# Sixteen units of a soft-routed MoE layer: the gated tile turned by a DMA transpose in f16 words instead of by TensorE in f32

## The chip, the cores and the metric

The kernel runs on one core of one Trainium2 chip. The metric is the device time of one execution in microseconds (us). The kernel before was timed three times: 547.62, 548.83 and 551.03 us, median 548.83 us. TensorE is called PE, VectorE DVE, ScalarE ACT, GpSimd POOL, and the queue on SyncE from which nearly all transfers are issued SP.

## The reference

Three layers follow one another, all in float32. Causal attention with decay over 4 batches x 8 heads x 576 positions x 64 gives x of 2304 tokens x 512. Layer 1 is a dense feed-forward layer with a sigmoid gate, and layer 2 a soft mixture of 8 experts with 4 slots each:

```python
h = x @ w_in                                  # 2304 x 2048
g = h * (1.0 / (1.0 + np.exp(-1.702 * h)))
y = g @ w_out                                 # 2304 x 512
logits = y @ phi                              # 2304 x 32
d = softmax(logits, over tokens); c = softmax(logits, over slots)
slot_input = d.T @ y                          # 32 x 512
slot_out[e] = relu(slot_input[e] @ w1[e]) @ w2[e]
out = c @ slot_out                            # 2304 x 512
```

## The kernel before, in words

**Layer 1 is folded.** y is never formed. The kernel computes `wphi = w_out @ phi` (2048 x 32) once, and the logits as `g @ wphi`; the sums over tokens are taken of g and multiplied by `w_out` at the end.

**Tiles.** The 2304 tokens are 18 blocks of 128; two blocks make a chunk, so there are nine chunks, 0 to 8. A chunk has eight units: a block `t` (0 or 1) and a group `fg` of 512 of the 2048 columns. In chunks 1 to 7 unit `u` is `t = u // 4`, `fg = u % 4`. A unit is twelve f16 matmuls of 512 columns into one PSUM bank `hp` (lines 814 to 816: high words times high, high times low, low times high, over four slices of 128), a Tanh on ACT into `g` (L829), and a multiplication on DVE (L830), which leaves the gated f32 tile `g`, 128 tokens x 512.

**The turn.** For the logits g must stand with its 512 columns on the partitions. `turn` transposes the four 128 x 128 pieces on PE in f32 against the identity (L766, `gT` in PSUM) and copies the result to SBUF on ACT (L773, `gt`, a ring of three tiles). `by_phi` then issues four f32 matmuls of `wphi` (32 columns) with `gt` (L788); each stands in the trace as two records, and piece `a` writes the partitions 32a to 32a+31 of the bank `p4`, so that four groups of PE columns are used. The 32-row groups are added up later by a matmul with `rsum` in `slot_steps`. A unit's `turn` is called in the step of the next unit or later, and its `by_phi` with the next `turn`, behind the last `hp` matmul issued.

**Attention runs between the units.** From row 5 on a piece of attention is: scores on PE (`scs`), a running maximum on DVE (L577), Exp on ACT (L581), normalisation into a high and a low f16 word, `pn`, on ACT and DVE (L589, L590), a DMA transpose from SP into `ph` (L594; most are 128x8x128, 128 partitions by eight blocks of 128), and then the products with the values on PE (`pv`, L632 to 634). Two `pn` tiles and three `ph` tiles rotate. The new row's q and k are turned by DMA transposes too (L347). `attn_items` gives each piece a place and a cost, and the main loop interleaves them with the units of layer 1 by goals; the tile framework then orders each engine's instructions by a simulated timeline. Each engine and the SP queue work strictly in that order.

**The end.** When attention's last item is issued its pool is closed and the expert weights of layer 2 are loaded from SP into the memory that has come free (L1109 onward, 127 transfers of 256 KB); PE works on chunks 7 and 8, and then on layer 2.

Of the kernel before, what the change touches and what calls it, by code (L numbers as in the profile page):

```python
# [10 lines left out]
F32 = mybir.dt.float32  # L11
F16 = mybir.dt.float16
BF16 = mybir.dt.bfloat16
U32 = mybir.dt.uint32
AF = mybir.ActivationFunctionType
# [15 lines left out]
def attention_moe_softmoe(ctx, tc, q, k, v, f, w_in, w_out, phi, w1, w2, out):  # L31
# [131 lines left out]
    w_at, w_loaded = [0], [0]  # L163
    W_AHEAD = 7

    N_LOW = 2
    RAW_AT = (7, 6, 5, 4, 3, None, None, 7, 6, None, None, 7, None, None, None, None)
    wo_pair = {}

# [28 lines left out]
    def w_first(n):  # L198


        if n in W32:
            nc.scalar.activation(out=W32[n], in_=W32[n], func=AF.Copy, scale=WS)
            return
        words = w_raw.pop(n).rearrange("p (n w) -> p n w", w=2)
        lo, hi = words[:, :, 0], words[:, :, 1]
        val = W32[n] = w32_tile(n)
        low = ap_.tile([128, 512], U32, tag="low", name="low", bufs=N_LOW)
        if n % 2 < 1:
            nc.gpsimd.tensor_scalar(out=val, in0=hi.bitcast(F32), scalar1=2.0 ** -111, scalar2=None, op0=ALU.mult)
        else:  # L210
            nc.scalar.activation(out=val, in_=hi.bitcast(F32), func=AF.Copy, scale=2.0 ** -111)
        nc.scalar.activation(out=low, in_=lo, func=AF.Copy, scale=0.93 * 2.0 ** -29)
        bits = val.bitcast(U32)
        nc.vector.scalar_tensor_tensor(
            out=low, in0=bits, scalar=3, in1=low, op0=ALU.logical_shift_left, op1=ALU.bitwise_or
        )
        nc.vector.scalar_tensor_tensor(
            out=bits, in0=bits, scalar=0x80000000, in1=low, op0=ALU.bitwise_and, op1=ALU.bitwise_or
        )
# [519 lines left out]

    G = {}
    P4 = {}
    held = deque()
# [6 lines left out]
    def units(c):  # L751
# [3 lines left out]
            return [(t, 2 * b + a) for b in range(2) for t in range(2) for a in range(2)]  # L755
        return [(t, fg) for t in range(2) for fg in range(FG)]

    def turn(c, t, fg):


        g = G[c, t, fg]
        pt = pt2 = ps_mm("gT")
        if (c, t, fg) == (NCH - 1, 1, FG - 1):
            pt2 = ps_sc("gT")
        for a in range(4):
            last_turn[0] = nc.tensor.transpose((pt if a < 2 else pt2)[:, a * 128:(a + 1) * 128], g[:, a * 128:(a + 1) * 128], ident)  # L766
        gt = mp.tile([128, 512], F32, tag="gt", name="gt", bufs=N_GT)
        if (c, t, fg) == (NCH - 1, 1, FG - 1):
            nc.scalar.copy(out=gt[:, halves[0]], in_=pt[:, halves[0]])
            nc.vector.tensor_copy(gt[:, halves[1]], pt2[:, halves[1]])  # L770
            warm(2)
        else:
            nc.scalar.copy(out=gt, in_=pt)  # L773
        with tc.issue_after(last_turn[0].ins):
            while held:
                by_phi(*held.popleft())
        held.append((c, t, fg, gt))
        if c == NCH - 1:
            by_phi(*held.popleft())

    def by_phi(c, t, fg, gt):
# [2 lines left out]
        if (t, fg) == first:  # L784
            P4[c, t if one else 0] = (ps_sc if one and t else ps_mi)("p4")
        p4 = P4[c, t if one else 0][:, 0 if one else 128 * t:][:, 0:128]
        for a in range(4):
            last_p4[0] = nc.tensor.matmul(  # L788
                p4[NS * a:NS * (a + 1)], lhsT=wphi[:, 4 * fg + a, :], rhs=gt[:, a * 128:(a + 1) * 128],
                start=((t, fg) == first), stop=(fg == FG - 1), skip_group_check=True,  # L790
# [9 lines left out]
    def moe_steps(c):  # L800
        xt = XT[c]
        for u, (t, fg) in enumerate(units(c)):
# [26 lines left out]
            nc.scalar.activation(out=g, in_=hp, func=AF.Tanh, scale=0.851 / (VS * WS))  # L829
            nc.vector.scalar_tensor_tensor(out=g, in0=g, scalar=1.0, in1=hp, op0=ALU.add, op1=ALU.mult)  # L830
            turns.append((c, t, fg))
            for _ in range(min(3 if c < 2 else 2, len(turns) - 1)):
                if turns[0][2] >= folded[0]:
                    break
                turn(*turns.popleft())
# [42 lines left out]
    def slot_steps(c, ts=(0, 1)):  # L878
# [3 lines left out]
        end = c == NCH - 1 and ts[-1] == 1  # L882
        l4 = mp.tile([128, 256], F32, tag="l4", name="l4", bufs=1)[:, 0:128 * nt]
        nc.vector.tensor_scalar(
            out=l4, in0=P4.pop((c, ts[0]))[:, 0:128 * nt], scalar1=1.0 / (GS * WS), scalar2=None, op0=ALU.mult
        )
        lg = ps_mi("lg")
        lT = lg[:, 0:128 * nt]
# [477 lines left out]
```

## Time and profile before

| | |
|---|---|
| median of three runs | 548.83 us |
| the profiled execution | 544.7 us, span of its instructions 542.2 us |
| PE busy | 492.7 us, 91% of the span |
| DVE busy | 350.4 us, 65% |
| ACT busy | 310.6 us, 57% |
| POOL busy | 71.5 us, 13% |
| granted TensorE clock, mean | 0.978 |
| bytes read from and written to HBM | 64.63 MB and 4.72 MB |

An engine's busy time is the union of its instructions in the trace. PE's matmuls are pipelined: one that lasts 0.38 us in the trace can start 0.22 us after the one before it. What a group of matmuls costs PE is therefore read from the starts: from its first start to the start of what follows. Chunks are found by the 72 Tanh instructions (L829), eight to a chunk: chunk 2's run from 189.7 to 227.3 us, chunk 4's from 272.6 to 310.5 us, chunk 6's from 364.6 to 404.9 us.

### The profile page before, as it was taken

Reading aid. Unit: us, or ns where it says so; the run is one execution under the profiler, and the core shown is the slowest. Engines: PE = TensorE matmul, PEld = TensorE weight load, DVE = VectorE, ACT = ScalarE, POOL = GpSimd, SP = SyncE. Lnnn points to the kernel's source line nnn. Section 1 sums busy time; section 2 is a strip of 40 time slices with the busy share of each in tenths; the row PEclk is TensorE's granted clock in tenths of the full one; section 3 lists DMA queues with packets and bytes.
Section 4 is the critical chain, followed back from the end, with each engine's and each line's share of the span. In section 5 each row is a group of like instructions: output and inputs, shape, how many; then the busy total and the mean of one; then the engine's idle time right before and its main releaser. Section 6 shows DMA issues by size and latency. Waiting matters only on the chain.

```text
span 542.2 us, 13552 instructions
## 1 busy us (share of the span) xinstructions
PE 492.7 (91%) x5353; PEld 309.1 (57%) x5353; DVE 350.4 (65%) x898; ACT 310.6 (57%) x607; POOL 71.5 (13%) x123
## 2 busy tenths in 40 slices
PE   3467899999889999999999999989999999999982
PEld 3456776866567555655665657556665555454531
DVE  8988979778666447667677868877675413360132
ACT  5867686778667446556666667576664323221211
POOL 4866754311000000010000001000000000000000
PEclk9969799999999999999999999999999999999997
DMA  9998763999959307997739699994554499989998
GB/s 242 285 376 149 200 129 133 272 191 204 169 105 168 61 19 139 185 181 139 125 77 181 116 189 176 212 156 88 93 105 90 132 383 367 348 308 367 337 327 269
DMA packets 230847, 105.62 MB, mean 195 GB/s; under 512 B 202593, under 2 KB 213345, under 8 KB 230785
## 3 DMA queue, kind: packets, MB, share of 16 engines
q1 hardware_dynamic: 229552, 103.59, 80.3%
q10 hardware_dynamic: 1232, 1.18, 0.7%
q8 instruction: 42, 0.69, 0.6%
q14 instruction: 21, 0.16, 0.1%
HBM read 64.63 MB, written 4.72 MB: 128 GB/s over the span
## 4 chain that ended last, share of the span: by engine, by line
PE 65%; DMA 15%; DVE 9%; ACT 4%; SPq 2%; issue 2%; POOL 0%; DVEq 0%; ACTq 0%; POOLq 0%
PE hp L814 10%; PE hp L815 9%; PE hp L816 9%; DMA ph<-pn 6%; PE gT L766 5%; PE p L788 4%; DMA we<-in_moe_w_dram 3%; PE pv L626 3%; PE l L1227 3%; PE sp L954 3%; PE pv L632 2%; DMA kf<-in_k_dram 2%; PE scs L554 2%; DMA kab<-kan 2%; PE scs L555 2%
## 5 line engine op out<-in xcount | busy, mean ns | idle before, releaser
L814 PE MATMUL hp<-w,xt 128*128 128x512 f16 x288 | 109.6, 381 | 0.6 <-DVE g L830 0.6
L815 PE MATMUL hp<-w,xt 128*128 128x512 f16 x288 | 109.2, 379 | 0.0
L816 PE MATMUL hp<-w,xt 128*128 128x512 f16 x288 | 109.2, 379 | 0.0
L581 ACT ACTIVATE pf<-scs,mx 128x512 f32<-128x512 f32 (+3 forms) x108 | 57.3, 541 | 38.7 <-DVE mx L577 29.4
L830 DVE SCALAR_TENSOR_TENSOR g<-g,hp 128x512 f32<-128x512 f32 x72 | 49.2, 683 | 43.9 <-ACT g L829 43.7
L590 DVE SCALAR_TENSOR_TENSOR pn<-pf,pn 128x512 f16<-128x512 f32 (+2 forms) x78 | 51.2, 658 | 32.1 <-ACT pn L589 31.4
L829 ACT ACTIVATE g<-hp 128x512 f32<-128x512 f32 x72 | 42.5, 590 | 47.4 <-PE hp L816 47.3
L589 ACT ACTIVATE pn<-pf 128x512 f16<-128x512 f32 (+2 forms) x78 | 47.3, 607 | 22.3 <-DMA ph<-pn 19.8
L577 DVE CUSTOM_DVE_ANT_0 scs<-scs,zmq 128x128 f32<-128x128 f32 (+3 forms) x96 | 46.6, 496 | 6.8 <-PE scs L555 4.2
L773 ACT COPY gt<-gT 128x512 f32<-128x512 f32 x71 | 41.1, 582 | 10.7 <-PE gT L766 10.5
L816 PEld LDWEIGHTS <-xt 128*128 128x128 f16 x288 | 28.2, 98 | 32.9
L632 PE MATMUL pv<-vv,ph 128*128 128x65 f16 (+1 forms) x360 | 41.8, 196 | 5.3 <-DMA ph<-pn 4.2
L814 PEld LDWEIGHTS <-xt 128*128 128x128 f16 x288 | 28.8, 100 | 28.8 <-issue 5.0
L766 PE MATMUL gT<-ident,g 128*128 128x128 f32 x288 | 45.0, 277 | 0.0
L766 PEld LDWEIGHTS gT<-ident,g 128*128 128x128 f32 x288 | 34.0, 141 | 14.8 <-issue 3.5
L632 PEld LDWEIGHTS <-ph 128*128 128x128 f16 (+1 forms) x360 | 33.8, 102 | 14.6 <-issue 7.0
L815 PEld LDWEIGHTS <-xt 128*128 128x128 f16 x288 | 28.2, 98 | 23.7 <-issue 1.1
L633 PE MATMUL pv<-vv,ph 128*128 128x65 f16 (+1 forms) x360 | 41.7, 195 | 0.0
L634 PE MATMUL pv<-vv,ph 128*128 128x65 f16 (+1 forms) x360 | 41.4, 194 | 0.0
L588 POOL MEMSET pn<- 128x128 f16 x12 | 2.5, 205 | 252.6 <-DMA ph<-pn 250.8
L633 PEld LDWEIGHTS <-ph 128*128 128x128 f16 (+1 forms) x360 | 34.1, 102 | 2.5 <-issue 0.6
L554 PE MATMUL scs<-kab,qa 128*128 128x128 f16 x240 | 34.4, 220 | 0.5 <-ACT pf L581 0.5
(233 smaller groups left out, 1017.3 us busy)
## 6 DMA issues: line engine op xcount, KB each, us to landing
we<-in_moe_w_dram SPq DMA_DIRECT2D x127, 256.0 KB, 5.5
raw<-in_moe_w_in_dram SPq DMA_DIRECT2D x16, 512.0 KB, 7.2
raw<-in_moe_w_out_dram SPq DMA_DIRECT2D x16, 512.0 KB, 5.7
kf<-in_k_dram SPq DMA_DIRECT2D x13, 256.0 KB, 3.3
qf<-in_q_dram SPq DMA_DIRECT2D x13, 256.0 KB, 3.7
vf<-in_v_dram SPq DMA_DIRECT2D x12, 256.0 KB, 4.2
out_dram<-ob SPq DMA_DIRECT2D x12, 256.0 KB, 3.5
ph<-pn SPq DMA_TRANSPOSE x78, 3.0
```

Source lines behind the costliest of these rows:

```text
L554: nc.tensor.matmul(o, lhsT=QA[r][:, h, :], rhs=KA[base + j][:, h, :], start=True, stop=False)
L577: nc.vector.tensor_tensor_reduce(out=o, in0=o, in1=mask, scale=-SC, scalar=3.0e38 if n == 128 else DG[r][1][:, u], op0=ALU.add, op1=ALU.mi ...
L581: nc.scalar.activation(out=pf[:, hh * nb:(hh + 1) * nb], in_=o, func=AF.Exp, bias=mx[:, hh:hh + 1], scale=-1.0)
L589: nc.scalar.activation(out=pn[:, 0, 0:w], in_=pf, func=AF.Copy, scale=PB)
L590: nc.vector.scalar_tensor_tensor(out=pn[:, 1, 0:w], in0=pf, scalar=PB, in1=pn[:, 0, 0:w], op0=ALU.mult, op1=ALU.subtract)
L632: nc.tensor.matmul(o, lhsT=ph[0:rr, 0, off:off + n], rhs=vh, start=(j == 0), stop=False)
L633: nc.tensor.matmul(o, lhsT=ph[0:rr, 0, off:off + n], rhs=vl, start=False, stop=False)
L766: last_turn[0] = nc.tensor.transpose((pt if a < 2 else pt2)[:, a * 128:(a + 1) * 128], g[:, a * 128:(a + 1) * 128], ident)
L814: nc.tensor.matmul(hp, lhsT=xt[:, 0, kk, ts], rhs=win(0, fg, kk), start=(kk == 0), stop=False)
L815: nc.tensor.matmul(hp, lhsT=xt[:, 0, kk, ts], rhs=win(1, fg, kk), start=False, stop=False)
L816: last_hp[0] = nc.tensor.matmul(hp, lhsT=xt[:, 1, kk, ts], rhs=win(0, fg, kk), start=False, stop=(kk == KD - 1))
L830: nc.vector.scalar_tensor_tensor(out=g, in0=g, scalar=1.0, in1=hp, op0=ALU.add, op1=ALU.mult)
```

## The change

In units 1, 2, 3, 5 and 6 of chunks 2 and 4 and units 1 to 6 of chunk 6 the turn is done another way. `stage`, called right behind the unit's L830, writes g times 2^-8 as a high and a low f16 word side by side into `gh` (one on ACT, one on DVE), and a DMA transpose from SP turns both words at once, 128x8x128, into `gt`. `turn` then issues no PE transpose and no ACT copy for that unit, but only the held `by_phi` of the unit before. `by_phi_halves` multiplies with f16 words of `wphi` (made once, `split_wphi`): two matmuls of 64 columns (g's high word with both words of wphi), four of 32 columns (g's low word with the high word of wphi), two of 64 columns. The other units of these chunks keep the PE transpose and scale by 2^-8 in the copy; the divisor in `slot_steps` takes the factor back. The two tiles of the tag `low` get tags of their own, `low0` and `low1`, which `gh` and the words of `wphi` use after them.

```diff
-        low = ap_.tile([128, 512], U32, tag="low", name="low", bufs=N_LOW)
+        low = ap_.tile([128, 512], U32, tag=f"low{n % 2}", name="low")
...
+    BY_DMA = {2: (1, 2, 3, 5, 6), 4: (1, 2, 3, 5, 6), 6: (1, 2, 3, 4, 5, 6)}
+    TS = 2.0 ** -8
+    wphl = []
+    staged = {}
...
+    def split_wphi():
+        wphl.append(ap_.tile([128, 512], F32, tag="low1", name="wphl").bitcast(F16).rearrange(
+            "p (k h s) -> p k h s", k=KF, h=2))
+        nc.scalar.activation(out=wphl[0][:, :, 0], in_=wphi, func=AF.Copy)
+        nc.vector.tensor_tensor(out=wphl[0][:, :, 1], in0=wphi, in1=wphl[0][:, :, 0], op=ALU.subtract)
+
+    def stage(c, t, fg):
+        g = G[c, t, fg]
+        gh = ap_.tile([128, 512], F32, tag="low0", name="gh").bitcast(F16).rearrange("p (h n) -> p h n", h=2)
+        nc.scalar.activation(out=gh[:, 0], in_=g, func=AF.Copy, scale=TS)
+        nc.vector.scalar_tensor_tensor(
+            out=gh[:, 1], in0=g, scalar=TS, in1=gh[:, 0], op0=ALU.mult, op1=ALU.subtract
+        )
+        gt = mp.tile([128, 512], F32, tag="gt", name="gt", bufs=N_GT).bitcast(F16)
+        nc.sync.dma_start_transpose(
+            out=gt.rearrange("p (a q) -> p a q", q=128), in_=gh.rearrange("p h n -> p (h n)")
+        )
+        staged[c, t, fg] = gt
+
+    def by_phi_halves(p4, fg, gt, stop):
+        gt = gt.rearrange("p (h a q) -> p h a q", h=2, a=4)
+        for both, a, g0 in ((1, 0, 0), (1, 1, 2), (0, 0, 0), (0, 1, 1), (0, 2, 2), (0, 3, 3), (1, 2, 0), (1, 3, 2)):
+            w = wphl[0][:, 4 * fg + a, 0:1 + both].rearrange("p h s -> p (h s)")
+            last_p4[0] = nc.tensor.matmul(
+                p4[NS * g0:NS * (g0 + 1 + both)], lhsT=w, rhs=gt[:, 1 - both, a],
+                start=False, stop=stop, skip_group_check=True,
+            )
+
     def turn(c, t, fg):
+        if (c, t, fg) in staged:
+            with tc.issue_after(last_hp[0].ins):
+                while held:
+                    by_phi(*held.popleft())
+            held.append((c, t, fg, staged.pop((c, t, fg))))
+            return
...
+        elif c in BY_DMA:
+            nc.scalar.activation(out=gt, in_=pt, func=AF.Copy, scale=TS)
...
-        for a in range(4):
+        if gt.dtype == F16:
+            by_phi_halves(p4, fg, gt, fg == FG - 1)
+        for a in range(4) if gt.dtype == F32 else ():
...
+            if u in BY_DMA.get(c, ()):
+                if not wphl:
+                    split_wphi()
+                stage(c, t, fg)
...
-            out=l4, in0=P4.pop((c, ts[0]))[:, 0:128 * nt], scalar1=1.0 / (GS * WS), scalar2=None, op0=ALU.mult
+            out=l4, in0=P4.pop((c, ts[0]))[:, 0:128 * nt], scalar1=1.0 / (GS * WS * (TS if c in BY_DMA else 1.0)),
+            scalar2=None, op0=ALU.mult
```

How the instructions move, at two places. The first is PE in chunk 6, at one of its units, before (`gT` is the PE transpose, `p` the product with `wphi`):

```order
L555 MATMUL scs<-kab,qb 128x128
L766 MATMUL gT<-ident,g 128x128 x4
L788 MATMUL p_5242<-gt,wphi 32x128 x4
L814 LDWEIGHTS xt
L814 MATMUL hp<-w,xt 128x512
```

And PE at a staged unit of chunk 2 in the changed program (`wphl` is the f16 words of `wphi`):

```order
L857 MATMUL hp<-w,xt 128x512
L784 LDWEIGHTS wphl
L784 MATMUL p_2916<-gt,wphl 64x128
L784 LDWEIGHTS wphl
L784 MATMUL p_2916<-gt,wphl 64x128
L784 LDWEIGHTS wphl
L784 MATMUL p_2916<-gt,wphl 32x128
...
L784 MATMUL p_2916<-gt,wphl 32x128
L784 LDWEIGHTS wphl
L784 MATMUL p_2916<-gt,wphl 64x128
L784 LDWEIGHTS wphl
L784 MATMUL p_2916<-gt,wphl 64x128
L564 LDWEIGHTS qa
```

The four transposes are gone, and the four f32 products have become eight f16 ones whose stationary tile changes from 64 to 32 columns and back. Over the program the PE transposes `gT` fall from 288 to 224, and 128 products with `wphl` come in. In five places other PE work now stands inside such a group of eight; the program before has two groups of `p` cut in the same chunks.

The second place is the SP queue in chunk 6, up to the first expert weights, before:

```order
L594 DMA_TRANSPOSE ph<-pn 128x6x128 x6
L347 DMA_TRANSPOSE qa<-qan 128x8x64
L347 DMA_TRANSPOSE qb<-qbn 128x8x64
L594 DMA_TRANSPOSE ph<-pn 128x6x128
L594 DMA_TRANSPOSE ph<-pn 128x8x128 x8
L594 DMA_TRANSPOSE ph<-pn 128x10x128 x4
L1109 DMA we<-in_moe_w_dram 128x512 x64
```

And in the changed program:

```order
L593 DMA_TRANSPOSE ph<-pn 128x6x128 x4
L775 DMA_TRANSPOSE gt<-gh 128x8x128
L593 DMA_TRANSPOSE ph<-pn 128x6x128 x2
L346 DMA_TRANSPOSE qa<-qan 128x8x64
L346 DMA_TRANSPOSE qb<-qbn 128x8x64
L775 DMA_TRANSPOSE gt<-gh 128x8x128
L593 DMA_TRANSPOSE ph<-pn 128x6x128 x2
L775 DMA_TRANSPOSE gt<-gh 128x8x128
L593 DMA_TRANSPOSE ph<-pn 128x8x128 x2
L775 DMA_TRANSPOSE gt<-gh 128x8x128
L593 DMA_TRANSPOSE ph<-pn 128x8x128 x3
L775 DMA_TRANSPOSE gt<-gh 128x8x128
```

The six new transposes stand one by one between attention's, and none stands behind the last `ph`, where the weights' loads begin.

## Rows read from the trace of the kernel before

**Rows 1.** Windows: length; busy us of PE, PEld, DVE, ACT, POOL; granted clock, DMA share, GB/s.

```profile
150.00:428.00 278.00, 272.33 (x3124) 166.98 (x3120) 189.97 (x526) 172.77 (x350) 5.56 (x32) 1.00 0.71 128
189.00:230.00 41.00, 41.00 (x486) 24.29 (x484) 23.76 (x63) 21.84 (x44) 0.82 (x4) 1.00 0.61 112
270.00:310.00 40.00, 39.44 (x446) 24.53 (x444) 30.26 (x81) 27.25 (x52) 0.00 (x0) 1.00 0.61 121
310.00:364.00 54.00, 51.15 (x605) 31.34 (x603) 41.00 (x126) 35.70 (x76) 2.34 (x13) 1.00 1.06 187
364.00:410.00 46.00, 45.78 (x557) 28.77 (x555) 33.15 (x87) 29.82 (x59) 0.62 (x3) 1.00 0.58 98
```

**Rows 2.** Waits of PE, 150 to 428 us: us in total, times, longest.

```profile
PE pv L632 <- DMA ph<-pn: 2.8, 4, 0.9
PE pv L632 <- DVE x L646: 1.1, 1, 1.1
```

**Rows 3.** Timeline of PE: start us, us, engine, line, operation.

```profile
202.03 0.65 PE L788 MATMUL p<-gt,wphi 128*32 128x128 f32 x16
202.60 0.30 PE L928 MATMUL d<-ident,dT 32*128 32x32 f32 x2
...
208.69 0.60 PE L766 MATMUL gT<-ident,g 128*128 128x128 f32 x4
209.22 0.43 PE L788 MATMUL p<-gt,wphi 128*32 128x128 f32 x8
209.58 0.20 PE L632 MATMUL pv<-vv,ph 128*128 128x65 f16 x1
...
210.41 0.22 PE L565 MATMUL scs<-kab,qa 128*64 128x128 f16 x2
210.47 0.22 PE L569 MATMUL scs<-kab,qb 128*64 128x128 f16 x2
210.62 0.39 PE L814 MATMUL hp<-w,xt 128*128 128x512 f16 x1
...
241.21 0.60 PE L766 MATMUL gT<-ident,g 128*128 128x128 f32 x4
241.64 0.38 PE L814 MATMUL hp<-w,xt 128*128 128x512 f16 x1
...
422.76 0.19 PE L634 MATMUL pv<-vv,ph 128*64 128x65 f16 x1
422.79 0.20 PE L632 MATMUL pv<-vv,ph 128*64 128x65 f16 x1
422.91 0.43 PE L788 MATMUL p<-gt,wphi 128*32 128x128 f32 x8
```

**Rows 4.** Groups by line and shape: busy us, mean ns; idle before.

```profile
L773 ACT COPY gt<-gT 128x512 f32<-128x512 f32 x71 | 41.1, 582 | 10.7 <-PE gT L766 10.5
L589 ACT ACTIVATE pn<-pf 128x512 f16<-128x512 f32 x42 | 26.4, 631 | 13.0 <-DMA ph<-pn 12.1
L590 DVE SCALAR_TENSOR_TENSOR pn<-pf,pn 128x512 f16<-128x512 f32 x42 | 28.9, 688 | 14.7 <-ACT pn L589 14.5
```

**Rows 5.** DMA issues: count, median us to landing.

```profile
ph<-pn SPq DMA_TRANSPOSE x78, 3.0
```

**Rows 6.** Timeline of the SP queue: start us, us of issue.

```profile
245.38 1.24 SPq L594 DMA_TRANSPOSE ph<-pn  x1
...
426.42 44.27 SPq L1109 DMA_DIRECT2D we<-in_moe_w_dram  x64
```

**Rows 7.** Waits of the SP queue, 150 to 428 us: us in total, times, longest.

```profile
SPq L594 <- DVE pn L590: 49.2, 32, 5.5
...
SPq L1109 <- DVE x L646: 6.3, 1, 6.3
```

**Rows 8.** The chain that ended last, near the end: start us, us, what.

```profile
506.31 4.31 DMA we<-in_moe_w_dram
510.68 7.71 DMA we<-in_moe_w_dram
```

More of the change, by code (lines that the diff above doesn't have):

```diff
@@ L164, in attention_moe_softmoe @@
     W_AHEAD = 7
-    N_LOW = 2
     RAW_AT = (7, 6, 5, 4, 3, None, None, 7, 6, None, None, 7, None, None, None, None)
```

## The prediction

> **What bounds the kernel now.** I read the windows first. From 150 to 428 us, attention and layer 1 interleaved, PE is busy 272.3 of 278 us at a granted clock of 1.00, the 2.4 GHz level [rows 1]. The staged units lie in the windows 189 to 230, 270 to 310 and 364 to 410 us (chunks 2, 4 and 6), where PE is busy 41.0 of 41, 39.4 of 40 and 45.8 of 46 us. The reader is to see that nothing else is near that: DVE has 23.8, 30.3 and 33.2 us, ACT 21.8, 27.3 and 29.8, and the DMA share is 0.61, 0.61 and 0.58. PE's waits agree: for attention's `ph` 2.8 us in four waits, for a DVE result 1.1 us [rows 2]. So time taken off PE here is time off the stretch, if no wait takes its place.
>
> Behind it stands a second bound. The expert weights are issued from 426.4 us on [rows 6], when SP's wait for attention's last `x` from DVE ends [rows 7], and the chain of waits near the end is made of these transfers (4.3 and 7.7 us pieces at 506 and 511 us) [rows 8]. Their start hangs on attention's last product on PE, so it moves with PE. In the changed order the last staged transpose stands ahead of the last `ph`, so it does not hold the loads. I carry what PE gains by 426 us through to the end, neither more nor less.
>
> **The transposes taken away.** From the first `gT` to what follows is 0.53 us when `p` follows (208.69 to 209.22) and 0.43 us when a full-width `hp` follows (241.21 to 241.64) [rows 3]. The 0.10 us between belongs not to the transposes but to a change of tile shape on PE: `pv` matmuls on 64 columns start 0.03 us apart, and a 32-column `p` starts 0.12 us after one (422.76, 422.79, 422.91); an `hp` starts 0.15 us after a pair of 64-column `scs` where a pair takes 0.06 us (210.41, 210.47, 210.62) [rows 3]. A change of shape thus costs 0.09 us, each way. In the changed program `p` still has to be entered from another shape, so I credit 0.43 us: 16 x 0.43 = 6.9 us.
>
> **The products made of other pieces.** Before, a unit's `p` costs 0.36 us (209.22 to 209.58), and two units in a row 0.57 us (202.03 to 202.60) [rows 3]. The second unit adds 0.21 us, 26 ns a record; leaving the shape is in the 0.36. The new eight: a pair of 64-column matmuls on the two halves of the array 0.06 us (as the `scs` pairs), a change to 32 columns 0.09, four 32-column ones at 26 ns 0.10, a change back 0.09, a pair 0.06, leaving 0.09. Sum 0.49 us, 0.13 more than before. The ends: if the two inner changes cost nothing, 0.31 us (0.05 less than before); if each of the eight takes a pair's 0.06 us and all three changes cost 0.09, 0.75 us (0.39 more). I take 0.13, since the one row in which a 32-column matmul follows a 64-column one shows the 0.09. The Trainium skill ("TensorE: Matmul & The Clock Gate", section "Measured speedup vs the span model") lets matmuls in distinct column groups overlap at about 4 ns each; by that the four would take some 0.07 us instead of 0.10 and the sum be 0.5 us better. The rows here show 26 ns a record, so I stay with them.
>
> Net per unit: -0.43 + 0.13 = -0.30 us (from -0.48 to -0.04); times 16, **-4.8 us** (from -7.7 to -0.6). In five places other work now splits a group of eight, before in two: three more changes of shape, **+0.3 us**.
>
> **What the other engines get.** ACT writes `gh`'s high word (0.63 us, as `pn`) in place of the copy of `gT` (0.58 us) [rows 4]: 16 x 0.05 = 0.8 us, hidden, since ACT is free for a third of these windows [rows 1]. DVE gets 16 low words at 0.69 us [rows 4], 11 us, and the words of `wphi` once; in chunk 6 that makes 33.2 + 6 x 0.69 = 37.3 of 46 us [rows 1], still covered by PE. If that cover went, the running maximum would be late next, and with it the scores' PSUM banks. The scale and the new divisor ride on instructions that are there already. Taking `gT` out also takes 16 tenants out of the PSUM ring that `hp` uses; PE hardly waits for that ring, so nothing is credited.
>
> **The queue.** A transpose of this shape holds SP 1.24 us [rows 6] and has landed after 3.0 us [rows 5]. Sixteen are 20 us of queue, five or six to a window: 5 x 1.24 = 6.2 us on 0.61 x 41 = 25 us makes 0.76, in chunk 4 0.77, in chunk 6 0.74. Each is also a place where the queue waits, for DVE's low word, with attention's `ph` and the next row's loads behind it. The one `gh` tile makes unit n+1's ACT word wait for unit n's transpose: 0.63 + 0.69 + 3.0 = 4.3 us a turn, against units some 5 us apart. The product of a staged unit stands on PE some two units or more behind its `hp`, which is 10 us against 4.3 us. PE's cost from all this: nothing at the low end, since SP itself waits 49.2 us for DVE's `pn` [rows 7], that is, the queue mostly runs ahead of its work. At the high end PE idles as it does where the transfers are full: between 310 and 364 us the DMA share is 1.06 and PE idles 2.85 of 54 us, 5.3% [rows 1]. On the 127 us of the three windows that is 6.7 us, less the 0.8 us there now: 5.9 us. The expected shares of 0.74 to 0.77 are nearer to 0.6 than to 1.06, so I take **+0.5 us**.
>
> **Sum:** -4.8 + 0.3 + 0.5 = -4.0 us. The profiled execution took 544.7 us, 4.1 us under the median of 548.8 us; the changed one would take 540.7 us by it, and the median would be **544.8 us**. About 1%, 5.5 us, is what a measurement of this kernel can tell from no change, so this is within it.
>
> **The rivals.**
>
> *Free inner changes, faster.* If PE starts a matmul of another width as soon as its columns are free, the products cost 0.31 us and the change gives -7.7 + 0.3 + 0.5 = -6.9 us: 541.9 us. For it: the two inner changes stay within one group of products and one PSUM bank, and the rows show changes only between groups. Against it: 422.79 to 422.91, where the columns of the other half were free as well [rows 3].
>
> *The gain comes back as waits, no change.* With PE idling at 5.3% in the three windows: -4.8 + 0.3 + 5.9 = +1.4 us, 550.2 us. For it: attention's ACT already waits for the transposes (13.0 us idle before L589, mostly for `ph`) [rows 4]. Against it: PE waited 2.8 us for `ph` in 278 us [rows 2].
>
> *The queue decides, slower.* If PE waits at each staged unit for an attention `ph` that stands behind the new transpose for the whole of its slot, that is 16 x 1.24 = 20 us, against a gain of 4.5 us: +15 us, 564 us. It decides from 0.62 us a unit on (0.28 us that eat the gain and 5.5 / 16 = 0.34 us more), half a slot. The DMA share and SP's own waits speak against it; the strict order of the queue, with a wait for DVE at the head of each new transpose, speaks for it. The Trainium skill ("VectorE: DVE Perf Modes", sections "The three transpose paths" and "Rules for kernel authors") has a rule against the whole change: turn 128x128 on TensorE if PSUM will do, at 390 ns against 1309 ns for the DMA; eight blocks by its figure would be an estimated 10.5 us a unit, and this rival would be sure. The trace disagrees for eight blocks in one transfer: 3.0 us to landing [rows 5].
>
> That the transposes stay on PE is excluded: the program's `gT` fall from 288 to 224.
>
> **Chances.** Forecast (543.3 to about 549 us) 0.49, free inner changes 0.29, gain lost in waits 0.13, queue decides 0.09. Faster by over 1% is the second alone, 0.29; within 1% the first and third, 0.62; slower by over 1% 0.09. The range reaches from the second's full gain (548.8 - 7.4 = 541.4 us without new waits) to a little past the third's 550.2 us: 541 to 551 us. Left out are the last rival and the far end of the second.
>
> **What would show it.** On PE's timeline: no `gT` before a group of `wphl` products, and from the group's first start to the next instruction 0.49 us; 0.31 us would be the free change, over 0.6 us the upper end. In the windows: PE still over 98% busy around the three chunks, DMA share near 0.75. In PE's waits: `ph` and `gt` together under 1.5 us more than now; several us there would be the third or fourth case. The start of the weights' loads should come 4 us earlier, at about 422 us, and the end with it. The forecast is wrong if the loads start earlier and the end does not move (then the tail has a bound that I did not see), or if the first 150 us, whose order the new tags of `low` shuffle a little, change by more than 1 us.

## The result and the profile after

The changed kernel took 554.18 us in the median (547.37 to 556.75, 18 runs), the kernel before 549.44 us on the same chip (547.09 to 552.89, 18 runs). The ratio is **1.0058 [1.0035, 1.0080]**: 3.2 us slower (1.9 to 4.4), where 4.0 us faster were forecast. The ratio leaves out five of the changed kernel's 18 runs, which were in a slower state; the two medians stand at 1.0086. The ratio is inside the 1% that the prediction takes for no change, but its interval leaves out 1, and 554.18 us lies outside the range of 541 to 551 us.

The profiled execution took 553.6 us with a span of 551.9 us. The profile shown of before is of an execution of 544.7 us, under all 18 of its timed runs, so the two profiles stand 8.9 us apart and the programs 3.2 us. They show where things happen; how much they are worth is read from the ratios.

| | before | after |
|---|---|---|
| first Tanh of chunk 2 | 189.7 | 192.6 us |
| first Tanh of chunk 4 | 272.6 | 275.1 us |
| first Tanh of chunk 6 | 364.6 | 371.1 us |
| Tanh of chunk 7, unit 4 | 430.7 | 441.6 us |
| expert weights issued from | 426.4 | 437.4 us |
| last Tanh to the end of the span | 66.7 | 65.5 us |
| PE busy, mean granted clock | 492.7, 0.978 | 496.9, 0.963 |

Windows of after, in columns as [rows 1]: the same stretches, moved with the chunks.

```profile
150.00:439.00 289.00, 275.29 (x3075) 164.34 (x3074) 199.55 (x543) 176.53 (x353) 5.55 (x32) 0.99 0.76 138
192.00:232.00 40.00, 38.16 (x448) 21.98 (x447) 24.67 (x59) 21.23 (x42) 0.82 (x4) 1.00 0.75 122
272.00:312.00 40.00, 37.16 (x381) 22.36 (x380) 29.33 (x75) 25.06 (x48) 0.00 (x0) 0.97 0.66 134
312.00:367.00 55.00, 52.82 (x636) 32.18 (x635) 42.16 (x130) 35.92 (x75) 2.31 (x13) 0.99 1.00 172
370.00:416.00 46.00, 41.01 (x507) 25.19 (x505) 35.85 (x92) 30.03 (x58) 0.42 (x2) 0.99 0.72 134
```

PE, full before in the three staged windows [rows 1], now idles 1.84, 2.84 and 4.99 us in them. The DMA share rose to 0.75, 0.66 and 0.72. DVE took up its low words and stays under PE (35.85 against 41.01 us in the last window). What PE idles for stands first in its waits, 150 to 439 us (total, times, longest), as [rows 2]:

```profile
PE pv L631 <- DMA ph<-pn: 11.8, 12, 2.8
```

Before it was 2.8 us in four waits. One profile's waits vary, but those of all the runs below agree: from 190 to 440 us PE waits 0.6 to 2.6 us for `ph` in the six profiles without a staged transpose, and 7.6 to 11.4 us in the five with all sixteen. The staged units are not what waits: no wait of PE for `gt` stands among them. Attention's products wait.

They need not wait for a `ph` that is itself held up behind a staged transpose. The `ph` that ends the longest wait was issued at 303.80 us, 0.06 us after its `pn` was done, and landed at 308.32, 4.5 us later, where 3.0 us is the median. (Landings of over 3.6 us are not new: 19 of 59 from 190 us on before, 20 of 60 now.) Its `pn` was late, since ACT had waited for an earlier `ph` to land:

```profile
302.38 0.63 ACT L588 ACTIVATE pn<-pf 128x512 f16<-128x512 f32 x1 [2.01 <-DMA ph<-pn]
```

That earlier `ph` had stood 1.6 us in the queue behind the new row's turns, and the one before it 5.5 us, behind a staged transpose among others. The `ph` of the second wait, of 2.08 us, was issued 0.07 us after its `pn` and landed after 4.7 us. So the delay behind the first wait came to PE through attention's rotating tiles, and no single transpose can be named for it.

The second loss is the clock. Two places of after, in windows of 4 us:

```profile
304.00:308.00 4.00, 1.53 (x32) 1.12 (x30) 2.22 (x4) 2.09 (x4) 0.00 (x0) 1.00 0.56 121
308.00:312.00 4.00, 3.63 (x35) 2.31 (x36) 2.61 (x6) 2.49 (x5) 0.00 (x0) 0.65 0.73 163
312.00:316.00 4.00, 4.00 (x18) 1.59 (x16) 2.33 (x4) 2.60 (x5) 0.00 (x0) 0.92 0.29 66
410.00:414.00 4.00, 1.17 (x30) 0.93 (x28) 2.43 (x7) 2.50 (x6) 0.00 (x0) 1.00 0.48 104
414.00:418.00 4.00, 4.00 (x50) 2.44 (x51) 3.24 (x7) 2.87 (x6) 0.42 (x2) 0.63 0.72 153
418.00:422.00 4.00, 4.00 (x36) 2.27 (x34) 1.13 (x4) 1.84 (x4) 0.41 (x2) 0.94 0.63 142
```

PE is busy 1.53 of 4 us, and the next window's granted clock is 0.65, that is, for most of it the lower level, 1.2 of 2.4 GHz. The same again at 410 us. On PE's timeline behind the first wait:

```profile
308.37 0.20 PE L631 MATMUL pv<-vv,ph 128*128 128x65 f16 x1 [2.84 <-DMA ph<-pn]
...
310.47 0.63 PE L855 MATMUL hp<-w,xt 128*128 128x512 f16 x1
310.89 0.63 PE L856 MATMUL hp<-w,xt 128*128 128x512 f16 x1
```

`hp` starts are 0.42 us apart here and 0.22 us at the full clock. Adding the busy time times one minus the granted clock over windows of 2 us, from 190 to 440 us, 3.3 us went this way in after and nothing before; PE's idle time went from 4.4 to 12.4 us. Such sums of one profile each are no price: the version of chunks 2 and 6 below, which is faster than before, has 1.7 and 11.9 us.

The edit itself did on PE what was foretold. A staged group, with what stands ahead of it and behind it:

```profile
230.41 0.38 PE L857 MATMUL hp<-w,xt 128*128 128x512 f16 x1
230.72 0.59 PE L784 MATMUL p<-gt,wphl 128*64 128x128 f16 x8
231.24 0.23 PE L553 MATMUL scs<-kab,qa 128*128 128x128 f16 x1
```

The eight products cost 0.52 us to the next start, 0.49 us in the prediction; the four `gT` are gone. The weights' loads, which were to come 4 us earlier, come 11 us later:

```profile
437.36 2.74 SPq L1155 DMA_DIRECT2D we<-in_moe_w_dram  x6
```

### The profile page after: what moved, and what is told of

Same layout as the page of the kernel before. It is cut to its first block, busy times and chain, and to the rows that moved or that the text cites. A ratio compares the mean times of both kernels' runs of the same rounds, so it can differ in the third digit from the quotient of the medians.

```text
span 551.9 us, 13490 instructions
## 1 busy us (share of the span) xinstructions
PE 496.9 (90%) x5289; PEld 307.3 (56%) x5289; DVE 360.0 (65%) x915; ACT 312.2 (57%) x608; POOL 71.9 (13%) x123
## 4 chain that ended last, share of the span: by engine, by line
PE 64%; DMA 16%; DVE 10%; ACT 5%; issue 2%; SPq 2%; DVEq 0%; ACTq 0%
DMA ph<-pn 10%; PE hp L855 10%; PE hp L856 9%; PE hp L857 9%; PE gT L803 3%; PE pv L625 3%; PE sp L1000 3%; PE p L829 3%; PE l L1273 3%; DMA we<-in_moe_w_dram 2%; PE pv L631 2%; DVE low L213 2%; PE scs L553 2%; PE scs L554 2%; PE pv L632 1%
## 5 line engine op out<-in xcount | busy, mean ns | idle before, releaser
L855 PE MATMUL hp<-w,xt 128*128 128x512 f16 x288 | 111.1, 386 | 0.0
L856 PE MATMUL hp<-w,xt 128*128 128x512 f16 x288 | 110.6, 384 | 0.0
L857 PE MATMUL hp<-w,xt 128*128 128x512 f16 x288 | 110.1, 382 | 0.0
L870 ACT ACTIVATE g<-hp 128x512 f32<-128x512 f32 x72 | 42.6, 591 | 49.2 <-PE hp L857 48.8
L631 PE MATMUL pv<-vv,ph 128*128 128x65 f16 (+1 forms) x360 | 42.7, 196 | 14.0 <-DMA ph<-pn 13.6
L576 DVE CUSTOM_DVE_ANT_0 scs<-scs,zmq 128x256 f32<-128x256 f32 (+3 forms) x96 | 46.5, 497 | 6.1 <-PE scs L554 4.6
L631 PEld LDWEIGHTS <-ph 128*128 128x128 f16 (+1 forms) x360 | 33.9, 102 | 24.6 <-DMA ph<-pn 17.9
L632 PE MATMUL pv<-vv,ph 128*128 128x65 f16 (+1 forms) x360 | 42.0, 195 | 0.0
L633 PE MATMUL pv<-vv,ph 128*128 128x65 f16 (+1 forms) x360 | 41.7, 195 | 0.0
L632 PEld LDWEIGHTS <-ph 128*128 128x128 f16 (+1 forms) x360 | 34.2, 103 | 3.5 <-issue 1.2
L803 PE MATMUL gT<-ident,g 128*128 128x128 f32 x224 | 34.9, 277 | 0.4 <-DVE g L871 0.4
L554 PE MATMUL scs<-kab,qb 128*128 128x128 f16 x240 | 34.6, 221 | 0.2 <-DMA qb<-qbn 0.2
L633 PEld LDWEIGHTS <-ph 128*128 128x128 f16 (+1 forms) x360 | 34.3, 103 | 0.8 <-issue 0.4
```

The source lines that it names most:

```text
L576: nc.vector.tensor_tensor_reduce(out=o, in0=o, in1=mask, scale=-SC, scalar=3.0e38 if n == 128 else DG[r][1][:, u], op0=ALU.add, op1=ALU.mi ...
L631: nc.tensor.matmul(o, lhsT=ph[0:rr, 0, off:off + n], rhs=vh, start=(j == 0), stop=False)
L632: nc.tensor.matmul(o, lhsT=ph[0:rr, 0, off:off + n], rhs=vl, start=False, stop=False)
L633: nc.tensor.matmul(o, lhsT=ph[0:rr, 1, off:off + n], rhs=vh, start=False, stop=(j == i))
L855: nc.tensor.matmul(hp, lhsT=xt[:, 0, kk, ts], rhs=win(0, fg, kk), start=(kk == 0), stop=False)
L856: nc.tensor.matmul(hp, lhsT=xt[:, 0, kk, ts], rhs=win(1, fg, kk), start=False, stop=False)
```

## The experiments

Each was timed in five rounds against the kernel before on its chip; a ratio stands with its 95% interval, and a difference of two ratios is uncertain by both. 1% is 5.5 us. The chip is the same within each group of runs below, but not from group to group.

### The parts of the change

**Tags alone:** the kernel before with one line changed.

```diff
-        low = ap_.tile([128, 512], U32, tag="low", name="low", bufs=N_LOW)
+        low = ap_.tile([128, 512], U32, tag=f"low{n % 2}", name="low")
```

> The kernel before with nothing but the two tags for the tiles of low: no staged unit, no new instruction, but the framework orders the first 190 us otherwise. Theory A (the new transposes stand in attention's way on the SP queue, PE waits for ph, and TensorE's clock falls behind the longer waits): no effect, ratio 0.998 to 1.002, since no transpose is added. Theory B (the loss comes from the changed order of the first 190 us, where the changed kernel's trace is 2.9 us behind at the first unit of chunk 2): ratio about 1.005, 2.9 us, and the first unit of chunk 2 some 3 us later than before.

Measured: 1.0060 [1.0033, 1.0088].

**PE's part alone:** the change without words and transposes; the staged products read the words of `wphi`, so a part of the logits is left out.

```diff
     def stage(c, t, fg):
-        g = G[c, t, fg]
...
-        staged[c, t, fg] = gt
+        staged[c, t, fg] = wphl[0].rearrange("p k h s -> p (k h s)")
```

> The changed kernel without the staging: no gh words on ACT and DVE and no DMA transpose; the sixteen units' f16 products read the words of wphi as their moving operand, so their share of the logits is left out of the computation. PE's work is that of the changed kernel. Theory A: PE's gain of 16 x 0.27 = 4.3 us stands by itself, ratio 0.991 to 0.994, waits of PE for ph in 150 to 440 us about 3 us as before. Theory B: the front still costs 2.9 us, so ratio 0.997 or so. Theory C (the extra ACT and DVE words make pn late): as theory A, ratio 0.992.

Measured: 0.9987 [0.9960, 1.0013].

**The load alone:** the change's words and transposes, read by nobody; every unit turned on PE in f32.

```diff
-        gt = mp.tile([128, 512], F32, tag="gt", name="gt", bufs=N_GT).bitcast(F16)
+        gt = ap_.tile([128, 512], F32, tag="low1", name="gtx").bitcast(F16)
...
-        staged[c, t, fg] = gt
...
```

> The kernel before with the sixteen stagings added to it (words on ACT and DVE and DMA transpose, into a tile that nobody reads) and every unit still turned on PE. Theory A: all of the cost and none of the gain, ratio 1.012 to 1.020 (7 to 11 us), PE's waits for ph in 150 to 440 us above 9 us. Theory B: about 3 us from the front and nothing from the staging, ratio 1.005. Theory C: as theory A.

Measured: 1.0142 [1.0106, 1.0178], PE's `ph` waits from 150 to 440 us 10.5 us.

**No transposes:** the change with the words on ACT and DVE, but the products read the words of `wphi` (a part of the logits is left out).

```diff
...
-        nc.sync.dma_start_transpose(
-            out=gt.rearrange("p (a q) -> p a q", q=128), in_=gh.rearrange("p h n -> p (h n)")
-        )
-        staged[c, t, fg] = gt
+        staged[c, t, fg] = wphl[0].rearrange("p k h s -> p (k h s)")
```

> The changed kernel with the words of g written on ACT and DVE but not transposed by DMA; the products read the words of wphi instead, so the sixteen units' share of the logits is left out of the computation. Theory A: the gain stands, as the queue is free: ratio 0.991 to 0.996, PE's waits for ph about 3 us. Theory C: the words alone make pn and ph late, so PE's waits for ph stay near 11 us and the ratio at 1.003 to 1.010. Theory B: ratio 0.997 to 1.000.

Measured: 0.9946 [0.9911, 0.9980], `ph` waits from 150 to 440 us 3.6 us.

What follows: theory B (the order of the front) has the first two runs, theory A (the transposes) the last two, and theory C falls, since the words on ACT and DVE cost nothing that can be seen. Without the transposes PE's saving is there: 0.73% between the first two runs, 4.0 us (1.9 to 6.1). The transposes take 0.82% (load alone against tags alone) to 1.12% (the change against no transposes): 4.5 us (2.0 to 7.0) and 6.1 us (3.9 to 8.4). And the new tags are no neutral part: alone they cost 0.6%. In the queue an attention `ph` then stands behind the next row's `qb`, `kf` and `qf` where it stood ahead of them; in its profile PE waits 2.8 us for a `ph` until 138.9 us, and the granted clock is 0.50 from 140 to 145 us, where before it was 1.00.

### With the order ahead of chunk 2 as before

The next four keep `low` a ring of two and put `gh` and `wphl` into it, which leaves every engine's order as before up to chunk 2.

**The ring:**

```diff
-        low = ap_.tile([128, 512], U32, tag=f"low{n % 2}", name="low")
+        low = ap_.tile([128, 512], U32, tag="low", name="low", bufs=2)
...
-        gh = ap_.tile([128, 512], F32, tag="low0", name="gh")...
+        gh = ap_.tile([128, 512], F32, tag="low", name="gh", bufs=2)...
```

> The changed kernel with the tiles of low back in one ring of two, from which the words of g and of wphi are taken afterwards: the order up to chunk 2 is then that of the kernel before, and all of the staging is there. Theory D (the front's lost order is one cost, 3.3 us; the queue's cost and PE's gain in the staged chunks cancel): ratio 0.997 to 1.003, first unit of chunk 2 at 189 to 190.5 us, PE's waits for ph after it still 9 us or more. Theory B alone (the front is all, the staging free): ratio 0.991 to 0.994. Theory A alone (the queue is all): ratio 1.005 as the changed kernel.

Measured: 1.0051 [1.0023, 1.0080].

**The ring, products grouped by width** (the 64-column four first):

```diff
-        for both, a, g0 in ((1, 0, 0), (1, 1, 2), (0, 0, 0), (0, 1, 1), (0, 2, 2), (0, 3, 3), (1, 2, 0), (1, 3, 2)):
+        for both, a, g0 in ((1, 0, 0), (1, 1, 2), (1, 2, 0), (1, 3, 2), (0, 0, 0), (0, 1, 1), (0, 2, 2), (0, 3, 3)):
```

> As the run with the ring, but the four 64-column products of a unit stand first and the four 32-column ones behind them, so that the shape changes once inside the group and not twice. If a change of shape costs 0.09 us wherever it stands, a group takes 0.43 us in place of 0.52, 1.4 us over sixteen units, ratio 0.0026 lower than the run with the ring. If waits for ph decide in these chunks, PE arrives earlier at the same waits, and the ratio is the same.

Measured: 1.0039 [1.0009, 1.0068].

**The ring, no transposes** (the edit of "no transposes" on the ring):

> The ring, the words of g on ACT and DVE, f16 products that read the words of wphi (the sixteen units' share of the logits is left out of the computation), and no DMA transpose. Theory D: PE's gain alone, ratio 0.990 to 0.994 (3.3 to 5.5 us), PE's waits for ph after 190 us 3 us or less. Theory C (the words on ACT and DVE make pn late): ratio near 1.000 with 9 us of waits.

Measured: 0.9885 [0.9842, 0.9927].

**The ring, load alone** (the edit of "load alone" on the ring):

> The ring, every unit turned on PE as before, and the sixteen stagings added with nobody reading the turned tile. Theory D: the queue's cost alone, ratio 1.006 to 1.011 (3.3 to 6 us), waits for ph after 190 us above 8 us. Theory B alone: ratio 0.998 to 1.002.

Measured: 1.0095 [1.0062, 1.0128].

What follows: with the front out of the comparison the transposes cost 1.66% (ring against ring without them, 9.1 us, 6.3 to 11.9) or 0.95% (load alone, 5.2 us, 3.4 to 7.0). Without them the kernel would be 6.3 us faster than before. The ring as a whole missed theory D's 0.997 to 1.003 and is no faster than the change (1.0051 against 1.0058), although the new tags cost 0.6% alone: that the tags' price is part of the 1.0058 is not shown, and stays open. In the ratio grouping by width can't be told from the order of the change. On PE's timeline it can: where a group is not split and the clock is full it takes 0.38 to 0.40 us, and on the ring without the grouping 0.50 to 0.53 at most places, so a change of width inside a group has its price.

### Which chunk pays

The grouped ring kernel with the staging in one place only; the table is the whole edit.

```diff
-    BY_DMA = {2: (1, 2, 3, 5, 6), 4: (1, 2, 3, 5, 6), 6: (1, 2, 3, 4, 5, 6)}
+    BY_DMA = {2: (1, 2, 3, 5, 6)}
```

> The grouped ring version with the staging in chunk 2's five units only; chunks 4 and 6 turn all units on PE in f32. All sixteen units together ran at 1.0039 of the kernel before. Theory A (a staged unit saves PE 0.27 to 0.39 us everywhere, and what it costs depends on where its transpose falls: between 190 and 230 us attention waits little for ph, so here the saving stays): 0.996 to 0.998, ph waits after 190 us at most 1 us above the kernel before. Theory B (the cost is the same for every unit, 0.13 us net): 1.0012, not to be told from 1. Theory C (one or two long ph waits with the clock's fall behind them, far from the staged units): not foretold by chunk, the three chunks need not add up to 1.0039.

Measured: 0.9974 [0.9943, 1.0004].

```diff
+    BY_DMA = {4: (1, 2, 3, 5, 6)}
```

> The grouped ring version with the staging in chunk 4's five units only. Theory A: the cost falls here, 1.001 to 1.004, and PE waits for ph 2 us or more between 270 and 315 us, the clock falling behind the longest of them. Theory B: 1.0012. Theory C: no longer wait than in the kernel before in that stretch, or one in a place that chunk 4 does not touch.

Measured: **1.0095** [1.0058, 1.0132].

```diff
+    BY_DMA = {6: (1, 2, 3, 4, 5, 6)}
```

> The grouped ring version with the staging in chunk 6's six units only. Theory A: most of the cost falls here, 1.002 to 1.006, and PE waits for ph 3 us or more between 364 and 420 us, with the clock at its lower level behind a wait of over 2 us; the weights' loads start later than in the kernel before. Theory B: 1.0015. Theory C: the chunk alone is free, 0.997.

Measured: **0.9958** [0.9931, 0.9985].

```diff
+    BY_DMA = {2: (1, 2, 3)}
```

> The grouped ring version with the staging in units 1, 2 and 3 of chunk 2 only. Theory A: three units save 0.27 to 0.39 us each and nothing waits: 0.998 to 0.9985, at the limit of what five rounds tell. Theory B: 1.0007. If it comes out above 1.003, the place of a transpose in the queue is not what decides.

Measured: 0.9989 [0.9963, 1.0014].

What follows: within the noise the three chunks add up (-0.26 + 0.95 - 0.42 = +0.27%, uncertain by 0.55, against +0.39% together), and the whole loss is chunk 4's. Theory A was right that the place decides. It was wrong on chunk 6, which it took for the dearest, and on chunk 4, where it had 0.1 to 0.4% and the clock's fall: with chunk 4 alone the clock is 1.00 from 190 to 440 us. B, the same price everywhere, falls. Chunks 2 and 6 gain 0.28 and 0.38 us a unit, of the 0.39 us that a grouped unit saves PE by the timeline, so there the transposes cost little; they were not timed there with and without transposes.

The DMA share does not tell chunk 4 from the others: 0.61, and 0.61 and 0.58 in chunks 2 and 6 before [rows 1]. Does the queue? The queue of **before** in chunk 4, start and issue time:

```profile
283.11 1.26 SPq L347 DMA_TRANSPOSE qa<-qan  x1
284.47 1.21 SPq L347 DMA_TRANSPOSE qb<-qbn  x1
285.74 0.57 SPq L307 DMA_DIRECT2D kf<-in_k_dram  x1
286.37 0.57 SPq L307 DMA_DIRECT2D qf<-in_q_dram  x1
286.98 1.70 SPq L307 DMA_DIRECT2D vf<-in_v_dram  x1
288.78 2.92 SPq L594 DMA_TRANSPOSE ph<-pn  x2
291.79 1.27 SPq L347 DMA_TRANSPOSE kab<-kan  x1
293.16 1.28 SPq L347 DMA_TRANSPOSE kab<-kbn  x1
294.54 14.04 SPq L594 DMA_TRANSPOSE ph<-pn  x7
```

and in chunk 6:

```profile
379.80 1.23 SPq L347 DMA_TRANSPOSE qb<-qbn  x1
381.13 31.23 SPq L594 DMA_TRANSPOSE ph<-pn  x12
```

In chunk 4 the turns and loads of the new rows fill it for eleven us on end, 283 to 294.5, each starting as the one before has been issued. In chunk 6 the last row is in at 381 us, and the queue waits for its work: 12 `ph` in 31 us. But in chunk 2 it is filled too, from 203.5 to 212.2 and from 217.9 to 229.5 us. The queue with **chunk 4 alone** staged:

```profile
285.71 1.24 SPq L775 DMA_TRANSPOSE gt<-gh  x1
287.06 1.22 SPq L593 DMA_TRANSPOSE ph<-pn  x1
288.38 1.22 SPq L346 DMA_TRANSPOSE qa<-qan  x1
...
292.22 1.25 SPq L306 DMA_DIRECT2D vf<-in_v_dram  x1
293.56 1.55 SPq L593 DMA_TRANSPOSE ph<-pn  x1
295.21 1.24 SPq L775 DMA_TRANSPOSE gt<-gh  x1
296.56 1.23 SPq L593 DMA_TRANSPOSE ph<-pn  x1
...
302.00 1.25 SPq L775 DMA_TRANSPOSE gt<-gh  x1
```

The queue now starts one transfer after another from 285.71 to 303 us without a gap of over 0.2 us. On DVE the second unit's low word is done early:

```profile
290.37 0.68 DVE L771 SCALAR_TENSOR_TENSOR gh<-g,gh 128x512 f16<-128x512 f32 x1
```

It is ready at 291.05 and issued at 295.21 us, so it waits 4.2 us not for its data but for the queue. But the same happens where the staging pays. With **chunk 6 alone** staged, the second unit's low word on DVE, and the queue:

```profile
384.87 0.69 DVE L771 SCALAR_TENSOR_TENSOR gh<-g,gh 128x512 f16<-128x512 f32 x1
```

```profile
387.11 1.22 SPq L346 DMA_TRANSPOSE qa<-qan  x1
388.38 1.26 SPq L346 DMA_TRANSPOSE qb<-qbn  x1
389.69 1.30 SPq L775 DMA_TRANSPOSE gt<-gh  x1
391.11 2.57 SPq L593 DMA_TRANSPOSE ph<-pn  x2
393.89 1.23 SPq L775 DMA_TRANSPOSE gt<-gh  x1
```

It is ready at 385.56 and issued at 389.69 us, 4.1 us later, and the queue runs back to back from 384.7 to 398.5 us. Added up, the staged transposes stand 6.3 us in the queue in chunk 4 (five), 6.3 us in chunk 6 (six) and 10.9 us in chunk 2 (five, longest 4.9). So neither a queue that runs back to back at the place nor the time that a transpose stands in it tells the dear chunk from the others.

One number of before does set chunk 4 apart, though three chunks don't show that it is the cause: how full the queue is. SP's issues take 26.8 of the 40 us of chunk 4's window [rows 1] and 46.9 of the 54 us behind it; in chunk 2 it is 21.7 of 41 us and 28.8 of the next 40, in chunk 6 25.9 of 46 us and 2.6 of the next 16.

There is a second difference. With chunk 6 alone the queue's other 383 transfers keep the order of before; with chunk 4 alone 10 of them stand elsewhere (counted as the fewest that have to be moved, tiles of one name taken as equal). With chunk 2 alone 5 do, and cost nothing.

### Is it chunk 4's queue?

**Chunks 2 and 6:**

```diff
+    BY_DMA = {2: (1, 2, 3, 5, 6), 6: (1, 2, 3, 4, 5, 6)}
```

> The grouped ring version with the staging in chunks 2 and 6 only, eleven units. If the chunks add up (0.9974 and 0.9958 alone): 0.993, faster than the kernel before by about 3.7 us. If chunk 2's reordering costs chunk 6 its gain: 0.997 to 1.000.

Measured: **0.9937 [0.9906, 0.9969]**, 3.5 us faster than the kernel before (544.47 against 547.88 us in the median), the sum of the chunks. It is faster although its profile has PE wait 5.9 us for `ph` from 190 to 440 us, 2.9 us of it at 304 us, in chunk 4, where it stages nothing.

**Chunk 4 without its transposes** (the edit of "no transposes" on chunk 4 alone):

> Chunk 4's five units with words and f16 products but no transposes (the products read the words of wphi, so a part of the logits is left out). Theory Q (the five transposes on the queue hold attention's ph back): 0.996 to 0.998, five units' saving of 0.27 to 0.39 us, ph waits of PE after 190 us under 4 us. Theory O (the order behind the units, which also changes here, in 9 places of the queue): 1.005 or more.

Measured: 0.9974 [0.9946, 1.0001]. PE's waits for `ph` from 270 to 440 us are, with the transposes and without:

```profile
PE pv L631 <- DMA ph<-pn: 8.6, 11, 1.8
```

```profile
PE scs L554 <- DMA qb<-qbn: 2.3, 1, 2.3
PE pv L631 <- DMA ph<-pn: 0.8, 1, 0.8
```

The wait for `qb` is new. Of the 8.6 us, 1.1 us come before the first staged transpose is issued.

**Chunk 4's transposes from ACT's queue:**

```diff
-        nc.sync.dma_start_transpose(
+        nc.scalar.dma_start_transpose(
```

> Chunk 4's five units as in the run of chunk 4 alone, the five transposes issued from ACT's queue. Theory S (the slot of 1.24 us on SP and its place ahead of attention's ph are what costs): under 1.002, though ACT then carries the issue, five times 1.2 us. Theory D (the transposes' transfers themselves slow attention's, whichever queue issues them) or theory O (the order): 1.006 to 1.012.

Measured: 1.0329 [1.0282, 1.0377].

What follows: five transposes turn 0.9974 into 1.0095, so they cost chunk 4 1.21%, 6.6 us (4.1 to 9.1), 1.3 us each, and the loss comes with them, as theory Q had it (the order changes without them too, by 8 of the queue's transfers in the count above). The third run missed both ranges (under 1.002; 1.006 to 1.012) and decides nothing between slot and transfer, since a new wait took its place. SP's longest wait in it, 275 to 335 us (total, times, longest), and ACT's timeline:

```profile
SPq L593 <- DMA gt<-gh: 23.9, 5, 6.0
```

```profile
293.94 0.21 ACT L964 ACTIVATE nm<-nm 128x1 f32<-128x1 f32 x1
300.33 1.26 ACTq L775 DMA_TRANSPOSE gt<-gh  x1
301.63 0.63 ACT L318 ACTIVATE kbn<-kf 128x512 f16<-128x512 f32 x1 [7.49 <-issue]
```

Each queue's transposes wait until the other's have landed: SP's `ph` lands at 300.26 us and ACT's transpose goes at 300.33; that one lands at 303.07, and SP's next `ph` goes at 303.21. So ACT stands still behind its transpose and SP in its turn. The Trainium skill ("DMA: Bandwidth & Descriptors", section "Latency and other measured facts") says that transposes of two queues must not be in flight together and that software has to put them one behind the other; the trace shows that the program does so, at 23.9 us in five waits.

### A backlog at one place?

**Units 1 to 3 of chunk 4:**

```diff
+    BY_DMA = {4: (1, 2, 3)}
```

> The grouped ring version with the staging in units 1, 2 and 3 of chunk 4 only, where the queue runs back to back from the first staged transpose to the third (285.7 to 303.4 us in the run of all five). Theory B (a backlog at this place): 1.004 to 1.009, PE's waits for ph 2 us or more between 280 and 320 us. Theory E (each of the five units costs the same, 1.9 us by 1.0095 and its saving is in that): 1.0057 for three units, so this run alone does not tell the two apart.

Measured: 1.0069 [1.0042, 1.0097].

**Units 5 and 6 of chunk 4:**

```diff
+    BY_DMA = {4: (5, 6)}
```

> The grouped ring version with the staging in units 5 and 6 of chunk 4 only. Theory B: 0.998 to 1.001, the two units keep their saving of 0.3 to 0.8 us. Theory E: 1.0038.

Measured: 1.0053 [1.0030, 1.0076].

**Chunks 2 and 6, and units 5 and 6 of chunk 4:**

```diff
+    BY_DMA = {2: (1, 2, 3, 5, 6), 4: (5, 6), 6: (1, 2, 3, 4, 5, 6)}
```

> Chunks 2 and 6 and units 5 and 6 of chunk 4, thirteen units. Theory B: 0.991 to 0.994, as good as chunks 2 and 6 alone (0.9937) or a little better. Theory E: 0.9975.

Measured: 1.0035 [1.0008, 1.0063].

What follows: theory B falls. Units 5 and 6, which issue later than the backlog shown above, pay about as much as the other three, and they take the whole gain of chunks 2 and 6 away (0.9937 to 1.0035). So chunk 4's price is not one pile-up at 285 us. Theory E, the same price for each of the five units, fits the first two runs (1.0057 and 1.0038 forecast) and not the third (0.9975). What all versions of chunk 4 with transposes from SP share is that the row traffic behind them moves (6 to 11 of the queue's transfers stand elsewhere) and that PE waits for `ph` in chunk 6 as well, also where they stage nothing there: 3.6, 1.7 and 2.1 us from 364 to 440 us with all five units, units 1 to 3 and units 5 and 6, and no wait before. How much of the 6.6 us is the 1.24 us slots and how much the order that they bring about is open: a version with the slots and the old order behind them was not tried.

## Why the prediction was wrong

**The step that failed is the queue's price, "+0.5 us".** It measured 4.5 to 9.1 us, by four comparisons with and without transposes; the forecast's high end was 5.9 us. The price was set by the DMA share, "nearer to 0.6 than to 1.06". That share is nearly the same in chunks 2, 4 and 6, and one loses 0.95% where the others gain 0.26 and 0.42%. The sum behind it also adds two different things: 6.2 us in which SP issues to 25 us in which the 16 DMA engines move data. How full the queue itself was, the prediction did not ask; it was 0.67 in chunk 4's window and 0.87 behind it. The sentence that the queue "mostly runs ahead of its work", from a total of 49.2 us of waiting over 278 us [rows 7], is an average over stages and does not hold from 283 to 294.5 us. That the transposes cost, and that they cost in chunk 4, is shown by the runs with and without them. By which path, the slots, the order behind them or the transfers, is open.

**No term stood for the clock.** In after each of the two longest waits was followed by a stretch at the lower level, which took another 1.6 and 1.7 us by the windows above. But this is no fixed part of the loss: with chunk 4 alone the clock stayed at 1.00 from 190 to 440 us and the loss was there. Nor does every such wait bring it down: 2.4 us for `ph` (units 1 to 3 of chunk 2) and 2.3 us for `qb` (chunk 4 without its transposes) left it at 1.00, and after 1.6 us (units 5 and 6 of chunk 4) 4 us show 0.67.

**PE's term was right, its parts in part by luck.** -0.27 us a unit by the timeline (0.52 us for the products, 0.49 predicted, against 0.36 before, and the 0.43 us of the transposes as credited), -4.3 us in all against -4.8. In time the change without its transposes gave 4.0 us (PE's part against the tags) and 6.3 us (on the ring; 4.0 to 8.6). Free inner changes of shape are not there: 0.52 us, not 0.31, and 0.43 where a 64-column `scs` follows. But the 26 ns a record were an average and not the distance of two starts. In a staged group the four 32-column products start 3 to 4 ns apart (230.894 to 230.904 us), and before, the f32 ones start 7 ns apart in fours, 0.11 to 0.13 us from one four to the next (202.03 to 202.60 us; [rows 3] shows the whole). From one width's first start to the next width's it is 0.17 to 0.18 us, where the sum had 0.15 for a pair and 0.19 for the four. So the pairs were put too low and the four too high.

**ACT and DVE at nothing** was right: with the words and without the transposes the kernel stands at 0.9946, 0.9885 and 0.9974 of before.

**The five split groups (+0.3 us)** are 0.05%, less than any interval here can show.

**"Carry what PE gains to the end"** was right in form: the weights' loads came 11 us late in the profile, the last Tanh as well, and the rest of the way to the end changed by 1.2 us. Only the sign at 426 us was wrong.

**The front.** The prediction named a change of over 1 us in the first 150 us as what would make it wrong. It came: chunk 2 starts 2.9 us later in after, and the tags alone cost 0.6%. Over all profiles, the five with the new tags have chunk 2's first Tanh at 192.6 to 196.4 us (mean 194.5), the fifteen with the old front at 189.1 to 194.0 (mean 191.2): some 3 us are the tags', and one execution can be off by as much. The prediction saw the new order of the front and put no term for it. Yet the ring, with the old front, is as slow as the change, so the front is not shown to be a cause of the 1.0058.

**The rivals.** "The gain comes back as waits" was nearest, at +1.4 us, where +3.2 us was measured; in the profile PE idled 9.7 us in the three windows instead of its 6.7. "The queue decides" asked for 0.62 us a unit; over sixteen units the transposes cost 0.28 to 0.57 us each, under it, but in chunk 4 1.3 us (0.8 to 1.8). That this is the size of a slot is not shown to be more than chance. It was right in one chunk of three, and was written as all or nothing. Together the two had a chance of 0.22.

## What to carry to other kernels

A new transfer has no one price: the same transpose cost 1.3 us in chunk 4 and little enough in chunks 2 and 6 for the change to pay there. The DMA share and a total of the queue's waits hid this; how full the issuing queue is at the place and behind it did not, though three chunks do not prove that it decides. Neither a back-to-back queue nor a transpose that waits in it was a sign of loss. So move work to a queue chunk by chunk and time each, since here one table held a gain (0.9937 with chunks 2 and 6) and a loss (1.0095 with chunk 4). And do not read a price from the waits of one profile: the version that gains has PE idle about as long as the one that loses.

## What had not been expected

- **The clock falls behind a wait of PE within a full stretch.** After waits of 2.84 and 2.08 us for `ph`, windows of 4 us show 0.65 and 0.63, and then 0.92 and 0.94. Before, with no wait over 1.1 us in [rows 2], the clock was 1.00 from 150 to 428 us. Other waits as long left it at 1.00.
- **A transpose on a second queue was dearer here than on a full one.** Moving five from SP to ACT made the kernel 2.3% slower yet (1.0095 to 1.0329), since the transposes of the two queues wait for each other.
- **Two units undo eleven.** Chunks 2 and 6 gain 0.63%, and units 5 and 6 of chunk 4 turn this into a loss of 0.35%. That the two cost more there (0.98%) than alone (0.53%) is within the noise.
